# QK-normalized attention and a PReLU MLP on one core: visits by batch replaced by one flat list of bursts

## The chip, the cores and the metric

One Trainium2 chip, one core. The metric is the time of one execution in device microseconds. Engines are named as the profile names them: PE is TensorE (PEld its weight loads), DVE is VectorE, ACT is ScalarE, POOL is GpSimd, SP is SyncE, which here only requests DMAs.

## The reference

```python
def rmsnorm(x, g):
    rms = np.sqrt(np.mean(x * x, axis=-1, keepdims=True) + 1e-06)
    return x / rms * g
q_n, k_n = (rmsnorm(q, g_q), rmsnorm(k, g_k))       # q, k, v: (8, 12, 448, 64)
scores = scale * np.matmul(q_n, k_n.transpose(0, 1, 3, 2))
scores = scores - np.max(scores, axis=-1, keepdims=True)
attn = np.exp(scores)
attn = attn / (np.sum(attn, axis=-1, keepdims=True) + 1e-09)
x = np.matmul(attn, v)      # heads of a token side by side: (3584, 768)
h = x @ w_in                # (768, 2048)
g = np.maximum(h, 0.0) + alpha * np.minimum(h, 0.0)
out = g @ w_out             # (2048, 768), float32
```

## The kernel before

Eight batches, and in each three **pairs**: a pair i holds heads 2i and 2i+1 and the two beside them in the other half of the heads, so four heads, two in each half of the partitions. Keys and tokens are cut into seven tiles of 64 (J = 7).

For a pair, `load_qk` fetches q and k (tile nat, SP's queue), `norm_sum` squares them (tile sq, GpSimd; in batch 0 ACT) and sums on VectorE (tile ss), `norm_root` takes the inverse root on ACT (tile rr), `norm_scale` multiplies (tile qs, GpSimd; in batch 0 VectorE), and `turn` transposes seven blocks on TensorE into PSUM (tile tps) and copies them on VectorE to qT or kT; the gain goes into kT's copy. `score` makes one tile of scores for four heads (tile sc, four matmuls, two PSUM buffers) and its exp on ACT (tile expT). `den` adds the exps of a pair up with ones (tile dn, 28 matmuls) and inverts by Ln and Exp on ACT (tile rden); `attv` makes the values (tile av, 28 matmuls) and VectorE multiplies them by rden into xT. tps, dn and av share one PSUM buffer of two banks (tag acc).

The MLP of a batch is 16 **ups** (`up`: six matmuls into tile hT, alpha times h on ACT into ah, the larger of both on VectorE into gT) and, for two batches together, 14 **downs** (`down`: 16 matmuls over gT into tile op, a copy on VectorE to osb, after every second one an output DMA on SP). hT and op share two PSUM buffers of one bank (tag mm). gT holds two batches side by side.

Each engine runs its instructions in the order in which they are written; the schedule is by hand. A batch is 15 visits. In a visit stand first the preparation of the next batch (list `before`), then denominators or values and up to two score tiles with their exps, then units of the MLP of the batch before, ups first and downs after them, doled out by their estimated cost (1.13 and 2.6). The weights are requested on GpSimd's queue in batch 0, cast from float32 on the way: w_in in six pieces of 128 rows, w_out in 16. After the last batch stand its 16 ups, and after them 8 downs.

## Time and profile before

| | us |
|---|---|
| median of 3 runs | 589.3 |
| lowest and highest | 586.72, 590.89 |
| the profiled execution | 587.75 |
| its span, first to last instruction | 586.0 |
| TensorE busy in it | 459.7 (78%) |
| ACT, VectorE, GpSimd busy | 286.5, 221.6, 164.1 |

The span is what the trace shows; the profiled execution's own time lies 1.75 us above it. A busy TensorE is not one at its peak: the end of a matmul is modelled, and matmuls overlap.

### The profile page before, as it was taken

The page shows a single profiled execution, that of the slowest core. Times are in us where ns is not written, and L with a number is a line of the kernel's source. Part 1 is how long each engine was busy: PE and PEld are TensorE (multiplying, and loading weights), DVE is VectorE, ACT ScalarE, POOL GpSimd, SP SyncE. Part 2 cuts the span into 40 slices and gives each one's busy share as a digit, 9 for nine tenths or more (in the row PEclk, how much of TensorE's full clock was granted, in tenths as well). Part 3 has the DMA queues.
Part 4 walks back from the last instruction along what each step waited for, and adds up shares of the span by engine and source line. Part 5 has one row for each costly group of instructions (what it writes and reads, how often), then busy time and mean ns, then how long its engine had stood idle before and what let it go on. Part 6 is the DMA issues. An engine that isn't in the chain of part 4 may idle for free.

```text
span 586.0 us, 9396 instructions
## 1 busy us (share of the span) xinstructions
PE 459.7 (78%) x4016; PEld 241.5 (41%) x4016; DVE 221.6 (38%) x314; ACT 286.5 (49%) x371; POOL 164.1 (28%) x128
## 2 busy tenths in 40 slices
PE   0232668988698985988969886988969889999996
PEld 0111343455244552445424552445424554455453
DVE  0374326532353223533254323543254223422431
ACT  2245358841565424753557415664367426862410
POOL 2166814520435004360164202560054300000000
PEclk9999899999889998999989998899989999999999
DMA  9999920311930119302443127401363121012013
GB/s 178 218 204 183 250 58 2 48 28 28 213 51 12 44 32 212 49 1 55 113 106 46 28 55 173 81 11 31 93 148 49 29 55 27 3 27 53 3 28 81
DMA packets 30298, 45.45 MB, mean 78 GB/s; under 512 B 5424, under 2 KB 25904, under 8 KB 30256
## 3 DMA queue, kind: packets, MB, share of 16 engines
q1 hardware_dynamic: 20688, 33.05, 23.5%
q0 software_dynamic: 9568, 11.80, 12.4%
q8 instruction: 31, 0.51, 0.4%
q14 instruction: 11, 0.09, 0.1%
HBM read 45.62 MB, written 11.01 MB: 97 GB/s over the span
## 4 chain that ended last, share of the span: by engine, by line
PE 52%; DVE 17%; ACT 11%; DMA 9%; SPq 5%; issue 3%; POOL 2%; POOLq 0%; DVEq 0%; ACTq 0%
PE op L250 26%; PE hT L233 12%; DMA nat<-in_k_dram 7%; DVE ss L120 5%; ACT expT L186 5%; PE dn L197 5%; ACT ah L241 5%; DVE gT L242 4%; PE av L215 4%; SPq L89 4%; PE tps L155 3%; PE sc L179 2%; DVE qT L162 2%; DVE osb L260 2%; POOL sq L119 2%
## 5 line engine op out<-in xcount | busy, mean ns | idle before, releaser
L186 ACT ACTIVATE expT<-sc,expb 128x896 f16<-128x896 f32 x168 | 160.1, 1002 | 86.8 <-PE sc L179 86.8
L233 PE MATMUL hT<-xT,w_in_sb 128*128 128x448 f16 x768 | 165.6, 367 | 39.6 <-DVE gT L242 38.6
L250 PE MATMUL op<-w_out_sb,gT 128*128 128x384 f16 x896 | 153.5, 326 | 2.2 <-DVE gT L242 2.2
L119 POOL TENSOR_TENSOR sq<-nat 128x896 f32<-128x896 f32 x42 | 70.1, 1678 | 237.5 <-DMA nat<-in_q_dram 188.6
L233 PEld LDWEIGHTS <-w_in_sb 128*128 128x128 f16 x768 | 75.0, 100 | 125.3 <-issue 69.5
L242 DVE TENSOR_TENSOR gT<-hT,ah 128x448 f16<-128x448 f32 x128 | 77.4, 622 | 110.5 <-ACT ah L241 109.4
L241 ACT ACTIVATE ah<-hT,alpha_sb 128x448 f16<-128x448 f32 x128 | 79.4, 635 | 70.8 <-PE hT L233 69.3
L250 PEld LDWEIGHTS <-gT 128*128 128x128 f16 x896 | 84.2, 98 | 69.0 <-issue 16.9
L142 POOL TENSOR_TENSOR qs<-nat,rr 128x896 f16<-128x896 f32 x42 | 70.9, 1712 | 60.3 <-ACT rr L134 42.0
L260 DVE COPY osb<-op 128x384 f32<-128x384 f32 x56 | 31.2, 558 | 146.9 <-PE op L250 146.9
L155 PE MATMUL tps<-ident,qs 128*128 128x128 f16 x336 | 29.1, 232 | 61.1 <-DVE qs L142 40.8
L205 ACT ACTIVATE rden<-dn 128x896 f32<-128x896 f32 x24 | 22.0, 917 | 92.3 <-PE dn L197 92.3
L120 DVE TENSOR_REDUCE ss<-sq 128x14 f32<-128x896 f32 x48 | 50.4, 1079 | 36.8 <-POOL sq L119 36.7
L179 PE MATMUL sc<-qT,kT 64*64 64x448 f16 x672 | 54.3, 381 | 5.5 <-ACT expT L186 4.7
L155 PEld LDWEIGHTS <-qs 128*128 128x128 f16 x336 | 23.3, 103 | 68.3 <-DVE qs L142 44.5
L197 PE MATMUL dn<-expT,ones 64*64 64x448 f16 x672 | 39.1, 370 | 10.9 <-DVE kT L164 10.9
L215 PE MATMUL av<-expT,vt 64*64 64x448 f16 x672 | 38.0, 364 | 2.1 <-ACT rden L205 1.3
L224 DVE TENSOR_TENSOR xT<-av,rden 128x896 f16<-128x896 f32 x24 | 26.1, 1089 | 26.6 <-PE av L215 26.6
L179 PEld LDWEIGHTS <-kT 64*64 64x64 f16 x672 | 18.2, 109 | 34.4 <-issue 27.8
L197 PEld LDWEIGHTS <-ones 64*64 64x64 f16 x672 | 22.1, 111 | 23.0 <-issue 13.9
L215 PEld LDWEIGHTS <-vt 64*64 64x64 f16 x672 | 18.9, 109 | 19.1 <-issue 10.0
L206 ACT ACTIVATE rden<-rden 128x896 f32<-128x896 f32 x24 | 22.8, 951 | 0.8
(20 smaller groups left out, 77.9 us busy)
## 6 DMA issues: line engine op xcount, KB each, us to landing
nat<-in_q_dram SPq DMA_DIRECT2D x48, 224.0 KB, 6.2
nat<-in_k_dram SPq DMA_DIRECT2D x48, 224.0 KB, 6.5
out_dram<-osb SPq DMA_DIRECT2D x56, 192.0 KB, 2.7
vt<-in_v_dram POOLq DMA_DIRECT2D x16, 336.0 KB, 5.4
w_in_sb<-in_moe_w_in_dram POOLq DMA_DIRECT2D x6, 512.0 KB, 9.5
w_out_sb<-in_moe_w_out_dram POOLq DMA_DIRECT2D x16, 192.0 KB, 8.4
gain<-in_g_q_dram SPq DMA_DIRECT2D x2, 0.2 KB, 10.1
gk<-in_g_k_dram SPq DMA_DIRECT2D x2, 0.2 KB, 10.3
```

The costliest lines, as they stand in the source:

```text
L119: nc.gpsimd.tensor_mul(out=sqf, in0=src, in1=src)
L120: nc.vector.tensor_reduce(out=ss[:, at].rearrange("p h j -> p (h j)").unsqueeze(2), in_=sq, axis=AXIS_X, op=ALU.add,)
L142: eng.tensor_mul(out=t.rearrange("p j h d -> p h j d"), in0=nat[b, i, nm], in1=rr[:, at].unsqueeze(3).broadcast_to((128, 2, J, D)),)
L155: nc.tensor.transpose(tp[:, j, :], src[:, j].rearrange("p h d -> p (h d)"), ident)
L179: nc.tensor.matmul(out=sc[ds(64 * g, 64), par, :S], lhsT=kT[ds(64 * par, 64), g, j, :], rhs=qT[ds(64 * par, 64), g].rearrange("p j c -> p ...
L186: nc.scalar.activation(out=expT[b, i][:, j], in_=sc[:, :, :S], func=AF.Exp, scale=QK_SCALE, bias=expb[:, 0:1],)
L197: nc.tensor.matmul(out=dn[ds(64 * par, 64), g, :S], lhsT=ones[ds(64 * g, 64), :], rhs=e[ds(64 * g, 64), j, par, :], start=(j == 0), stop=( ...
L215: nc.tensor.matmul(out=av[ds(64 * par, 64), g, :S], lhsT=vt[b][ds(64 * g, 64), 2 * i + par, j, :], rhs=e[ds(64 * g, 64), j, par, :], start ...
L233: nc.tensor.matmul(out=hT[:, :S], lhsT=w_in_sb[:, c, ts(ft, 128)], rhs=x[:, c, :], start=(c == 0), stop=(c == KM - 1),)
L241: nc.scalar.activation(out=ah, in_=hT[:, :S], func=AF.Copy, scale=alpha_sb[:, ft : ft + 1])
L242: nc.vector.tensor_max(out=gT[:, ft, ds((b & 1) * S, S)], in0=hT[:, :S], in1=ah)
L250: nc.tensor.matmul(out=op[:, :OH], lhsT=gT[:, ft, ts(t, 128)], rhs=w_out_sb[:, ft, ds(oh * OH, OH)], start=(ft == 0), stop=(ft == NF - 1),)
```

## The change

The loops over batches and visits go. There are 24 pairs y in one line, 168 score tiles, and 84 **bursts** n. A burst holds, in this order: preparation due at n; the scores of tiles 2n and 2n+1; the exp of the first; denominators or values, if due (denominators one burst after the pair's last score tile, values two after); a turn, if due; then the burst's **gap**, a list of ups and downs. The exp of the second tile, and with denominators the inversion, are written behind the gap's first up, or at the gap's end if it has none. Loads stand 12 bursts ahead of the pair's first scores, squares 6, reduces 5, the root 4, the scale 3, the turn 1. `turn` makes q and k in the two banks of one buffer. In the MLP downs stand between ups, evenly spread. Of a pair of batches' downs, six are done in the odd batch's period and eight in the next one's; after the last burst stand 16 ups and 14 downs. In batch 0 GpSimd scales k, VectorE q. w_in is requested in four pieces of 512 columns, w_out in four of 512 rows.

```diff
-    def load_qk(b, i):
+    def load_qk(y):
+        b, i = divmod(y, G)
         for nm in "qk":
-            t = ld.tile([128, 2, J, D], FP32, name="nat", tag="nat", bufs=8)
+            t = ld.tile([128, 2, J, D], FP32, name="nat", tag="nat", bufs=6)
             for g in range(2):
...
-            nat[b, i, nm] = t
+            nat[y, nm] = t
...
+    def load_w_in(c):
+        nc.gpsimd.dma_start(
+            out=w_in_sb[:, :, ts(c, FB)],
+            in_=moe_w_in[:, ts(c, FB)].rearrange("(k p) f -> p k f", p=128),
+        )
+
+    def load_w_out(c):
+        nc.gpsimd.dma_start(
+            out=w_out_sb[:, ts(c, NF // 4), :],
+            in_=moe_w_out[ts(c, DF // 4), :].rearrange("(t p) m -> p t m", p=128),
+        )
+
+
+    def square(y, nm):
+        src = nat[y, nm].rearrange("p h j d -> p (h j d)")
         sq = ld.tile([128, 2 * J, D], FP32, name="sq", tag="sq", bufs=2)
         sqf = sq.rearrange("p n d -> p (n d)")
-        if fast:
+        if y < G:
             nc.scalar.activation(out=sqf, in_=src, func=AF.Square)
         else:
             nc.gpsimd.tensor_mul(out=sqf, in0=src, in1=src)
+        sqs[y, nm] = sq
+
+    def reduce(y, nm):
+        if nm == "q":
+            ss_t[y] = ld.tile([128, 2, 2, J], FP32, name="ss", tag="ss", bufs=4)
         nc.vector.tensor_reduce(
-            out=ss[:, at].rearrange("p h j -> p (h j)").unsqueeze(2),
-            in_=sq, axis=AXIS_X, op=ALU.add,
-        )
-
...
+    def root(y):
+        rr = ld.tile([128, 2, 2, J], FP32, name="rr", tag="rr", bufs=4)
+        nc.scalar.activation(out=rr, in_=ss_t[y], func=AF.Ln, scale=1.0 / D, bias=epsb[:, 0:1])
         nc.scalar.activation(out=rr, in_=rr, func=AF.Exp, scale=-0.5)
-        rr_t[key] = rr
-
...
+    def scale(y, nm):
         t = ld.tile([128, J, 2, D], FP16, name="qs", tag="qs", bufs=4)
-        eng = nc.vector if fast else nc.gpsimd
+        eng = nc.vector if y < G and nm == "q" else nc.gpsimd
         eng.tensor_mul(
             out=t.rearrange("p j h d -> p h j d"),
-            in0=nat[b, i, nm],
-            in1=rr[:, at].unsqueeze(3).broadcast_to((128, 2, J, D)),
-        )
...
+        qs[y, nm] = t
+
+    def turn(y):
 
         ps = psa.tile([128, 2, 512], FP32, name="tps", tag="acc")
-        tp = ps[:, 0, : S].bitcast(FP16).rearrange("p (j c) -> p j c", j=J)
-        src = qs[b, i, nm]
...
+        for n, nm in enumerate("qk"):
+            tp = ps[:, n, : S].bitcast(FP16).rearrange("p (j c) -> p j c", j=J)
+            for j in range(J):
+                nc.tensor.transpose(
+                    tp[:, j, :], qs[y, nm][:, j].rearrange("p h d -> p (h d)"), ident
+                )
+            t = att.tile([128, 2, J, 64], FP16, name=f"{nm}T", tag=f"{nm}T", bufs=3)
+            o = t.rearrange("p g j c -> p j g c")
+            i4 = tp.rearrange("p j (g c) -> p j g c", g=2)
...
+            qkT[y, nm] = t
...
+    def score(y, j):
+        qT, kT = qkT[y, "q"], qkT[y, "k"]
         sc = pss.tile([128, 2, 512], FP32, name="sc", tag="sc")
...
+        scs[y, j] = sc
+
+    def soft(y, j):
+        if j == 0:
+            expT[y] = att.tile([128, J, 2, S], FP16, name="expT", tag="expT")
         nc.scalar.activation(
-            out=expT[b, i][:, j], in_=sc[:, :, :S], func=AF.Exp,
...
+    def over_keys(name, y, weights):
+        acc = psa.tile([128, 2, 512], FP32, name=name, tag="acc")
...
+        return acc
+
+    def den(y):
+        dn = over_keys("dn", y, lambda g, par, j: ones[ds(64 * g, 64), :])
+        rden[y] = dn
+
+    def invert(y):
         r = att.tile([128, 2, S], FP32, name="rden", tag="rden")
-        nc.scalar.activation(out=r, in_=dn[:, :, :S], func=AF.Ln)
...
+        rden[y] = r
+
+    def attv(y):
+        b, i = divmod(y, G)
+        vv = vt[b]
+        av = over_keys("av", y, lambda g, par, j: vv[ds(64 * g, 64), 2 * i + par, j, :])
...
+    NB = (NG * J + 1) // 2
+
+    def last(y):
+        return (J * y + J - 1) // 2
+
+    dens = {last(y) + 1: y for y in range(NG)}
+    avs = {last(y) + 2: y for y in range(NG)}
+    prep = {}
+
+    def at(n, f, *a):
+        prep.setdefault(max(int(n), 0), []).append((f, a))
+
+    for y in range(G, NG):
+        n = J * y / 2
+        at(n - 12, load_qk, y)
+        for nm in "qk":
+            at(n - 6, square, y, nm)
+            at(n - 5, reduce, y, nm)
+        at(n - 4, root, y)
+        for nm in "qk":
+            at(n - 3, scale, y, nm)
+    for b in range(1, B):
+        at(J * G * b / 2 - 4, load_v, b)
+    turns = {J * y // 2 - 1: y for y in range(1, NG)}
+
+    UP, DOWN = 1.13, 2.6
+
+    def merge(ups, downs):
+        res, done = [], 0
+        for n, u in enumerate(ups):
+            while done < len(downs) and done * len(ups) <= n * len(downs):
+                res.append(downs[done])
+                done += 1
+            res.append(u)
+        return res + downs[done:]
+
+    periods = []
+    for b in range(B):
+        ups = [(UP, up, (b, ft)) for ft in range(NF)]
+        lead, downs = [], []
+        if b > 0 and b % 2 == 0:
+            lead = [(DOWN, down, (b - 2, 3, oh)) for oh in range(2)]
+            downs = [(DOWN, down, (b - 2, t, oh)) for t in range(4, J) for oh in range(2)]
+        elif b > 0:
+            downs = [(DOWN, down, (b - 1, t, oh)) for t in range(3) for oh in range(2)]
+        periods.append(lead + merge(ups, downs))
+    gaps = [[] for _ in range(NB + 2)]
+    for b in range(B - 1):
+        lo = last(G * b + G - 1) + 2
+        hi = last(G * b + 2 * G - 1) + 2
+        total = sum(u[0] for u in periods[b])
+        done, n = 0.0, lo
+        for u in periods[b]:
+            gaps[min(lo + int(done / total * (hi - lo) + 0.3), hi - 1)].append(u[1:])
+            done += u[0]
+    rest = [u[1:] for u in periods[B - 1]]
+    rest += [(down, (B - 2, t, oh)) for t in range(3, J) for oh in range(2)]
...
+    def prepare(y):
+        for nm in "qk":
+            square(y, nm)
+            reduce(y, nm)
+        root(y)
+        for nm in "qk":
+            scale(y, nm)
+
+    prepare(0)
+    nc.vector.tensor_mul(out=gain, in0=gain, in1=gk2)
+    turn(0)
+    prepare(1)
     load_v(0)
-    def prep_fast(i):
...
-        visits = [[] for _ in range(15)]
-        for i in range(G):
-            for n in range(4):
-                for j in range(2 * n, min(2 * n + 2, J)):
-                    visits[4 * i + n].append((score, (b, i, j)))
-            visits[4 * i + 5].insert(0, (den, (b, i)))
-            visits[4 * i + 6].insert(0, (attv, (b, i)))
-        visits[13] = [(den, (b, G - 1))]
-        visits[14] = [(attv, (b, G - 1))]
...
+    at(1, prepare, 2)
+    for c in range(4):
+        at(1 + c // 2, load_w_in, c)
+        at(8 + 2 * c, load_w_out, c)
+
+    for n in range(NB + 2):
+        for f, a in prep.get(n, ()):
+            f(*a)
+        tiles = [divmod(m, J) for m in (2 * n, 2 * n + 1) if m < NG * J]
+        for t in tiles:
+            score(*t)
+        if tiles:
+            soft(*tiles[0])
+        if n in dens:
+            den(dens[n])
+        if n in avs:
+            attv(avs[n])
+        late = [(soft, t) for t in tiles[1:]]
+        if n in dens:
+            late.append((invert, (dens[n],)))
+        if n in turns:
+            turn(turns[n])
+        for f, a in gaps[n]:
+            f(*a)
+            if f is up and late:
+                for g, c in late:
+                    g(*c)
+                late = []
+        for g, c in late:
+            g(*c)
+    for f, a in rest:
+        f(*a)
```

The gaps of 22 bursts, worked out from this code (U an up, D a down, both with no number; den, av, turn: what else the burst holds beside its two score tiles); bursts 23 to 43 repeat three times to the end:

```
12 av U U | 13 turn U | 14 den U U | 15 av U | 16 turn U U | 17 U U | 18 den U
19 av U U | 20 turn U | 21 den U U | 22 av D
23 turn U U U | 24 D | 25 den U U U | 26 av D | 27 turn U U D | 28 den U
29 av U U D | 30 turn U U | 31 U D | 32 den U U | 33 av D D | 34 turn D
35 den U U U | 36 av D U | 37 turn U U D | 38 U U D | 39 den U U | 40 av U D
41 turn U U U | 42 den D U U | 43 av D
```

On ACT, where a period of ups begins (batch 2 of before). hT, ah and rows of alpha belong to ups, sc and expT to score tiles, the number behind a name tells buffers apart:

```order
L186 ACTIVATE expT_1392<-sc_1393,expb_79 128x896
L186 ACTIVATE expT_1392<-sc_1399,expb_79 128x896
L241 ACTIVATE ah_1412<-hT_1405,alpha_sb_92 128x448
L241 ACTIVATE ah_1422<-hT_1415,alpha_sb_92 128x448
L241 ACTIVATE ah_1432<-hT_1425,alpha_sb_92 128x448
L186 ACTIVATE expT_1392<-sc_1442,expb_79 128x896
L186 ACTIVATE expT_1392<-sc_1448,expb_79 128x896
L241 ACTIVATE ah_1461<-hT_1454,alpha_sb_92 128x448
```

and in the new order, bursts 18 and 19, each with one or two ups:

```order
L193 ACTIVATE expT_941<-sc_961,expb_79 128x896
L246 ACTIVATE ah_1008<-hT_1001,alpha_sb_92 128x448
L193 ACTIVATE expT_941<-sc_966,expb_79 128x896
L219 ACTIVATE rden_1012<-dn_972 128x896
L220 ACTIVATE rden_1012<-rden_1012 128x896
L193 ACTIVATE expT_941<-sc_1024,expb_79 128x896
L246 ACTIVATE ah_1072<-hT_1065,alpha_sb_92 128x448
L193 ACTIVATE expT_941<-sc_1029,expb_79 128x896
```

Before, both exps of a visit stand together and the ups' steps behind them; now an up's step stands between the two exps, and in a burst with denominators the inversion (rden) stands behind the second.

On VectorE, a period of a batch before (ss<-sq is a reduce for the next batch, gT the end of an up, osb the end of a down):

```order
L224 TENSOR_TENSOR xT<-av,rden 128x2x448
L260 COPY osb<-op 128x384
L242 TENSOR_TENSOR gT<-hT,ah 128x448 x3
L120 TENSOR_REDUCE ss<-sq 128x14 x2
L242 TENSOR_TENSOR gT<-hT,ah 128x448 x4
L120 TENSOR_REDUCE ss<-sq 128x14 x2
L242 TENSOR_TENSOR gT<-hT,ah 128x448 x5
L120 TENSOR_REDUCE ss<-sq 128x14 x2
L242 TENSOR_TENSOR gT<-hT,ah 128x448 x2
L224 TENSOR_TENSOR xT<-av,rden 128x2x448
L242 TENSOR_TENSOR gT<-hT,ah 128x448 x2
```

and now, from burst 29 to burst 33:

```order
L229 TENSOR_TENSOR xT<-av,rden 128x2x448
L247 TENSOR_TENSOR gT<-hT,ah 128x448 x2
L265 COPY osb<-op 128x384
L132 TENSOR_REDUCE ss<-sq 128x14 x2
L166 COPY qT<-tps 128x7x2x64
L168 TENSOR_SCALAR kT<-tps,gain 128x7x2x64
L247 TENSOR_TENSOR gT<-hT,ah 128x448 x3
L265 COPY osb<-op 128x384
L247 TENSOR_TENSOR gT<-hT,ah 128x448 x2
L132 TENSOR_REDUCE ss<-sq 128x14 x2
L229 TENSOR_TENSOR xT<-av,rden 128x2x448
```

Three pairs of reduces between 14 gT have become one pair in every three or four bursts, and osb stands among gT.

On GpSimd, the start of the program before (vt, w_in_sb, w_out_sb are DMA requests):

```order
L98 DMA vt<-in_v_dram 64x6x448 x2
L330 DMA w_in_sb<-in_moe_w_in_dram 128x2048 x2
L119 TENSOR_TENSOR sq<-nat 128x896 x2
L330 DMA w_in_sb<-in_moe_w_in_dram 128x2048 x4
L119 TENSOR_TENSOR sq<-nat 128x896 x2
L339 DMA w_out_sb<-in_moe_w_out_dram 128x768 x6
L119 TENSOR_TENSOR sq<-nat 128x896 x2
L339 DMA w_out_sb<-in_moe_w_out_dram 128x768 x6
```

and now:

```order
L146 TENSOR_TENSOR qs<-nat,rr 128x2x7x64 x2
L101 DMA vt<-in_v_dram 64x6x448 x2
L146 TENSOR_TENSOR qs<-nat,rr 128x2x7x64
L107 DMA w_in_sb<-in_moe_w_in_dram 128x6x512 x4
L126 TENSOR_TENSOR sq<-nat 128x896 x2
L101 DMA vt<-in_v_dram 64x6x448 x2
L146 TENSOR_TENSOR qs<-nat,rr 128x2x7x64 x2
L126 TENSOR_TENSOR sq<-nat 128x896 x2
L113 DMA w_out_sb<-in_moe_w_out_dram 128x4x768 x2
```

The requests for v and w_in have moved behind the scales of k (qs) for the first two and the third pair.

## Rows read from the trace of the kernel before

**Rows 1.** Two stretches parted at the first up matmul: busy time by engine, clock, DMA.

```profile
0.00:87.80 87.80, 31.74 (x345) 18.47 (x345) 32.25 (x37) 33.99 (x43) 39.78 (x46) 0.96 0.89 182
87.80:586.00 498.20, 427.95 (x3676) 223.02 (x3672) 189.35 (x278) 252.54 (x329) 124.27 (x82) 0.97 0.27 59
```

**Rows 2.** What TensorE waited for from 87.8 us on: us, times, longest.

```profile
PE hT L233 <- DVE gT L242: 38.6, 36, 6.6
...
PE tps L155 <- DVE qT L162: 14.2, 18, 0.8
...
PE dn L197 <- DVE kT L164: 9.3, 12, 0.8
```

**Rows 3.** Head in order of time: start, us, engine, line, operation [idle before, releaser].

```profile
6.08 0.95 ACT L117 ACTIVATE sq<-nat 128x896 f32<-128x896 f32 x1 [4.07 <-DMA nat<-in_q_dram]
...
11.21 0.95 ACT L117 ACTIVATE sq<-nat 128x896 f32<-128x896 f32 x1 [4.17 <-DMA nat<-in_k_dram]
...
16.29 0.16 DVE L275 TENSOR_TENSOR gain<-gain,gk 128x1 f32<-128x1 f32 x1 [15.29 <-DMA gk<-in_g_k_dram]
...
16.37 2.07 DVE L120 TENSOR_REDUCE ss<-sq 128x14 f32<-128x896 f32 x2
...
20.23 0.93 PE L155 MATMUL tps<-ident,qs 128*128 128x128 f16 x7 [20.23 <-DVE qs L142]
...
24.20 3.70 ACT L186 ACTIVATE expT<-sc,expb 128x896 f16<-128x896 f32 x4 [5.15 <-PE sc L179]
```

**Rows 4.** One stretch of the head, columns as in group 1.

```profile
20.00:40.00 20.00, 5.87 (x48) 3.58 (x52) 10.99 (x12) 6.14 (x8) 12.01 (x14) 1.00 1.00 198
```

**Rows 5.** Order of time, middle of the program, downs between attention work.

```profile
394.36 1.52 PE L197 MATMUL dn<-expT,ones 64*64 64x448 f16 x28 [0.78 <-DVE kT L164]
...
395.68 0.57 PE L179 MATMUL sc<-qT,kT 64*64 64x448 f16 x8
...
400.24 0.55 PE L179 MATMUL sc<-qT,kT 64*64 64x448 f16 x8
...
400.72 2.77 PE L250 MATMUL op<-w_out_sb,gT 128*128 128x384 f16 x16
...
403.33 0.55 PE L155 MATMUL tps<-ident,qs 128*128 128x128 f16 x7
```

**Rows 6.** Order of time, ups in the tail.

```profile
538.67 2.43 PE L233 MATMUL hT<-xT,w_in_sb 128*128 128x448 f16 x12
...
540.01 0.63 ACT L241 ACTIVATE ah<-hT,alpha_sb 128x448 f16<-128x448 f32 x1 [6.08 <-PE hT L233]
...
540.68 0.62 DVE L242 TENSOR_TENSOR gT<-hT,ah 128x448 f16<-128x448 f32 x1 [1.24 <-ACT ah L241]
...
541.14 0.63 ACT L241 ACTIVATE ah<-hT,alpha_sb 128x448 f16<-128x448 f32 x1 [0.50 <-PE hT L233]
...
541.36 2.43 PE L233 MATMUL hT<-xT,w_in_sb 128*128 128x448 f16 x12 [0.25 <-DVE gT L242]
```

**Rows 7.** Order of time, the last copy of the output.

```profile
581.09 0.56 DVE L260 COPY osb<-op 128x384 f32<-128x384 f32 x1 [2.04 <-PE op L250]
```

**Rows 8.** Groups of instructions by line: busy us, mean ns, idle before.

```profile
L186 ACT ACTIVATE expT<-sc,expb 128x896 f16<-128x896 f32 x168 | 160.1, 1002 | 86.8 <-PE sc L179 86.8
...
L206 ACT ACTIVATE rden<-rden 128x896 f32<-128x896 f32 x24 | 22.8, 951 | 0.8
...
L205 ACT ACTIVATE rden<-dn 128x896 f32<-128x896 f32 x24 | 22.0, 917 | 92.3 <-PE dn L197 92.3
```

**Rows 9.** Order of time, start of a period.

```profile
364.33 1.08 DVE L120 TENSOR_REDUCE ss<-sq 128x14 f32<-128x896 f32 x1 [1.03 <-POOL sq L119]
...
366.00 4.06 PE L233 MATMUL hT<-xT,w_in_sb 128*128 128x448 f16 x12 [5.54 <-DVE gT L242]
```

**Rows 10.** Two stretches, columns as in group 1: ordinary ups, ups after an idle.

```profile
100.00:150.00 50.00, 43.69 (x432) 23.92 (x425) 19.31 (x30) 27.08 (x35) 14.11 (x10) 1.00 0.20 39
...
366.00:369.00 3.00, 3.00 (x9) 1.23 (x9) 0.47 (x1) 0.56 (x1) 2.83 (x2) 0.50 0.99 220
```

More of the change, by code (lines that the diff above doesn't have):

```diff
@@ L46 @@
     W = 2 * S
+    NG = B * G
+    FB = DF // 4
     cst = ctx.enter_context(tc.tile_pool(name="cst", bufs=1))
@@ L170 @@
-    expT, rden = {}, {}
-    def score(b, i, j):
-        if j == 0:
-            expT[b, i] = att.tile([128, J, 2, S], FP16, name="expT", tag="expT")
-        qT, kT = qkT[b, i, "q"], qkT[b, i, "k"]
+        for n, nm in enumerate("qk"):
[7 more added lines that the diff above has]
+            i4 = tp.rearrange("p j (g c) -> p j g c", g=2)
+            if nm == "q":
+                nc.vector.tensor_copy(out=o, in_=i4)
+            else:
+                nc.vector.tensor_scalar(
+                    out=o, in0=i4, scalar1=gain[:, 0:1], scalar2=None, op0=ALU.mult
+                )
+            qkT[y, nm] = t
@@ L176, in score @@
+    expT, rden, scs = {}, {}, {}
+    def score(y, j):
+        qT, kT = qkT[y, "q"], qkT[y, "k"]
         sc = pss.tile([128, 2, 512], FP32, name="sc", tag="sc")
@@ L197, in den @@
                     nc.tensor.matmul(
-                        out=dn[ds(64 * par, 64), g, :S],
-                        lhsT=ones[ds(64 * g, 64), :],
+                        out=acc[ds(64 * par, 64), g, :S],
+                        lhsT=weights(g, par, j),
                         rhs=e[ds(64 * g, 64), j, par, :],
@@ L203, in den @@
                     )
+        return acc
[3 more added lines that the diff above has]
+    def invert(y):
         r = att.tile([128, 2, S], FP32, name="rden", tag="rden")
-        nc.scalar.activation(out=r, in_=dn[:, :, :S], func=AF.Ln)
+        nc.scalar.activation(out=r, in_=rden[y][:, :, :S], func=AF.Ln)
         nc.scalar.activation(out=r, in_=r, func=AF.Exp, scale=-1.0)
-        rden[b, i] = r
-    def attv(b, i):
-        av = psa.tile([128, 2, 512], FP32, name="av", tag="acc")
-        e = expT[b, i]
-        for j in range(J):
-            for g in range(2):
-                for par in range(2):
-                    nc.tensor.matmul(
-                        out=av[ds(64 * par, 64), g, :S],
-                        lhsT=vt[b][ds(64 * g, 64), 2 * i + par, j, :],
-                        rhs=e[ds(64 * g, 64), j, par, :],
-                        start=(j == 0),
-                        stop=(j == J - 1),
-                    )
+        rden[y] = r
[3 more added lines that the diff above has]
+        av = over_keys("av", y, lambda g, par, j: vv[ds(64 * g, 64), 2 * i + par, j, :])
         if i == 0:
@@ L224, in attv @@
         nc.vector.tensor_mul(
-            out=xT[b][:, :, i, :], in0=av[:, :, :S], in1=rden[b, i]
+            out=xT[b][:, :, i, :], in0=av[:, :, :S], in1=rden[y]
         )
@@ L270 @@
         nc.sync.dma_start(out=gk2[ds(64 * g, 64)], in_=g_k.unsqueeze(1))
-    load_qk(0, 1)
-    load_qk(0, 2)
+    load_qk(1)
+    load_qk(2)
     nc.sync.dma_start(out=alpha_sb, in_=moe_alpha.rearrange("(t p) -> p t", p=128))
-    load_v(0)
-    nc.vector.tensor_mul(out=gain, in0=gain, in1=gk2)
-    def prep_fast(i):
-        for nm in "qk":
-            norm_sum(0, i, nm, True)
-        norm_root(0, i, True)
-        for nm in "qk":
-            norm_scale(0, i, nm, True)
-        for nm in "qk":
-            turn(0, i, nm)
```

112 lines of the change are left out of this document (10 added, 102 removed).

## Prediction

> **What bounds the kernel now.** I parted the execution at the first matmul of the MLP's first half, an "up", at 87.8 us [rows 1]. Before it TensorE is busy 31.7 of 87.8 us while the DMA engines are busy 0.89 of the time; after it TensorE is busy 428.0 of 498.2 us and DMA 0.27. So there are two kernels here: a head that waits, and a long part in which TensorE is the bound and loses 70 us.
>
> The table of waits says for what TensorE waits in the long part [rows 2]: 38.6 us before ups, for gT of an earlier up (that frees the up's PSUM buffer); 14.2 us in the middle of a turn, where k's transposes wait for q's copy; 9.3 us where denominators wait for k's copy. All three are waits for VectorE on buffers of PSUM.
>
> In the head I read the rows in order of time [rows 3]. q of pair 0 is squared at 6.08 us, k only at 11.21, 4.17 us late by its DMA; the gain product holds VectorE until 16.29, so the two reduces behind it start at 16.37 although k's square ended at 12.16; transposes at 20.23, first exps at 24.20. The DMA engines are full meanwhile [rows 4], because GpSimd requests v and a third of w_in while q and k are still to come.
>
> Now the price of dense work, read as the distance from one start to the next where nothing waits [rows 5]: 28 matmuls of denominators 1.32 us (394.36 to 395.68), a pair of score tiles 0.48 (400.24 to 400.72), a down 2.61 (400.72 to 403.33), seven transposes about 0.5 (0.55 with their tail). An up is 1.13: of two in a row the second's ACT step starts 1.13 after the first's [rows 6]. The whole program holds 128 ups (144.6), 56 downs (146.2), 84 pairs of score tiles (40.3), 48 sets of denominators or values (63.4), 48 half turns (24): 418.5 us. What is done before the first up is 10.5 pairs, 6 sets and 12 half turns (18.9) now, and will be 13 pairs, 6 sets and 8 half turns (18.1): 400 us of dense work stand behind the first up in both. From the last matmul to the end it is 5.1 us: the last copy starts at 581.09, 0.2 after its matmuls [rows 7]. So before is 87.8 + 400 + 5 = 493, and **93 us of its 586.0 are waits behind the first up** (65 of them plain idle, the rest half-speed matmuls and the refilling of the pipeline after each wait).
>
> **The change, part by part.** *Head.* GpSimd now scales k of pairs 0 and 1 before it requests v, and k of pair 2 before w_in, so q and k of batch 0 have the DMA engines alone. The least: k's square follows q's at 7.0, 4.2 us earlier, and without the gain's hold the reduces start 5.2 us earlier than k's square allowed, exps at 14.8; but ACT now also does pair 1's root ahead of the first exp, for which two reduces of 1.08 and the two small root steps (together 0.6, an estimate from ACT's other rows) must pass, so 17.5. The most: the gain's DMAs, issued at the same place, land as late as now, at 16.29; two copies (1.3) and the same 2.7 behind it give 20.4. I take 18.5. Then ACT sets the pace up to burst 12: 24 exps at 0.93 [rows 3], three inversions of 0.92 + 0.95 [rows 8], pair 2's two squares (1.9) with its reduce and root (1.7), two more roots (1.2): 32.7, then a pair of scores and the values (1.8): 53. TensorE is at its lower clock level there by its durations (seven transposes in 0.93 at 20.23 against 0.55 later [rows 3, 5]), though the granted clock shows 1.00; if it stays there, its 13 pairs, 6 sets and 8 half turns take 36 instead of 18 us and press on ACT: up to 60. Bounds 50 to 60, **first up at 54** instead of 87.8. w_in's first quarter must be there by then: at 198 GB/s [rows 4] 10 MB can have moved, and q and k of three pairs, v, two later pairs and that quarter are about 7.
>
> *Squares and reduces.* Today a load, its square and its reduce are handed out within two visits. At 364.33 VectorE stands at a reduce, waiting for GpSimd, which waited for a DMA; two gT stand behind it, and TensorE idles 5.54 us; the two ups after that take 4.06 instead of 2.44 [rows 9], because the granted clock is at 0.50, the lower level [rows 10]. Five period starts show the same, with 3.8 to 6.6 us of idle. Now loads go out 12 bursts ahead, squares 6 and reduces 5. Even in the full head k's first load had landed by 11.21 [rows 3]; six bursts are 30 us. So these waits go whole, and nothing takes their place on VectorE: a reduce's square is a burst old.
>
> *Turn.* q and k are turned into two banks of one buffer, so k's 14 us of waits for q's copy go, and units stand behind a turn, not denominators, which takes the 9 us.
>
> *Ups between downs, exps between ups.* Here the new waits come. An up's buffer is free 1.56 us after its end: 0.21 to ACT, 0.63, 0.04, 0.62 on VectorE, 0.06 back [rows 6]. With two buffers a unit directly behind two ups waits 1.56 - 1.13 = 0.43. In the 21 bursts of two batches (the list of gaps) that is 8 times: 3.4 us. **The late exp** is what the change adds: the second tile's exp stands behind the first up's ACT step. It ends 0.21 + 0.63 + 1.00 = 1.84 after that up, and the next burst's second score tile wants its buffer 0.24 after the gap's end. If the first up is also the gap's last unit (bursts 28, 36) TensorE waits 1.6: 3.2; if one up follows (bursts 30, 32, 39, 42), 0.47, four times: 1.9. In a denominator burst the Ln stands behind that late exp too and ends 2.8 after the first up; the values that need its buffer then wait 0.7, four times: 2.8. Twice a second up's ACT step stands behind both inversion steps and the next down waits 0.6: 1.1. Together 12 us for two batches, three times 12. The first period, ups alone, has four lone ups (6.4), four of the 0.47 kind and four of the 0.7 kind: 11. In the tail five triples of ups: 2. **Waits behind the first up 50** instead of 93. The least is half of them (25), if exps and evictions slip into other gaps; the most 80, if the waits of one burst carry into the next.
>
> *Without cost:* six downs go from the middle into the tail, dense in both; 14 more root steps on ACT (0.6 each) lie where ACT has room: two batches, some 115 us, hold 42 exps of 1.00, 32 ACT steps of ups of 0.63 and 12 inversion steps of 0.93 [rows 6, 8], 73 us. SP's outputs stand behind far-ahead loads, which wait for a scale one or two bursts earlier; three output buffers cover that.
>
> **Sum:** 54 + 400 + 50 + 5 = 509 us of span. The profiled execution has 587.75 for 586.0 of span, so 511; it lies 1.5 below the median of 589.3, which I leave out.
>
> **The rivals.** *ACT becomes the bound of the bursts.* Exp, up, exp, up in one queue could string each burst along ACT, and as much wait would stand behind the first up as now, 93: 54 + 400 + 93 + 5 + 2 = 554. For: every gap has its exp behind an up. Against: ACT's 73 us of 115, above.
>
> *The weights come late.* w_in is requested only when pair 2 is scaled, some 24 us in, in rows of 2 KB instead of 8. If that halved the rate, the first up would stand at 70 to 88: 527 to 545. Against: only a quarter is needed at first.
>
> *Slower: the clock falls.* The new order breaks TensorE's work into bursts with a short wait in nearly each; if the granted clock then went to its lower level, each us of dense work would cost another. From 80 us of such work on, a fifth of the 400, the gain is gone and the kernel is slower: at a third, 511 + 133 = 644. Against: in 100 to 150 us, where ups wait for gT by fractions of a us, 1.00 was granted [rows 10], and 0.50 came after an idle of over 5 us. The Trainium skill (TensorE: Matmul & The Clock Gate, "A second HAM failure mode: psum-queue depth-cycling") tells of a kernel whose short idles between groups of matmuls, as it cycled through PSUM, did make the clock swing; by this rule the rival would hold, and this trace does not agree with it at waits under 1 us.
>
> *Better:* 25 us of waits and a first up at 50 give 482.
>
> **How the numbers follow.** Chances: forecast with its bounds (486 to 536) 0.74; ACT-bound 0.08; late weights 0.08; better 0.05; slower 0.04; none of these, within 1%, 0.01. The range reaches to half of the late weights, 486 to 540. The runs of before lie 0.7% apart, so 1% is about what a measurement can tell. Faster by over 1% holds in all but the last two: 0.95, same 0.01, slower 0.04.
>
> **What would show it.** First up near 54, with k's first square right behind q's; no reduce that holds gT; no wait inside a turn; 58 us for each batch in the middle; among TensorE's waits the largest new entry scores for expT, some 20 to 25 us in all, then values for rden; a granted clock of 1.00 from 60 us on. I am wrong if scores wait for exps in bursts with several ups, if ups wait for w_in, or if the clock dips in the middle.

## The result and the profile after

| | before | after | forecast |
|---|---|---|---|
| median, us | 589.3 | **552.0** | 511 |
| lowest, highest | 586.7, 590.9 | 550.2, 555.2 | 486 to 540 |
| profiled execution, its span | 587.75, 586.0 | 552.83, 551.1 | 511, 509 |
| first up | 87.8 | 58.4 | 54 |

The ratio is 0.938 [0.932, 0.943]: the change gains 37 us of the 78 that were forecast, and the time lies above the range. Two stretches of the changed kernel, parted at its first up (columns as in [rows 1]):

```profile
0.00:58.40 58.40, 29.48 (x329) 15.55 (x330) 24.82 (x29) 37.36 (x48) 33.30 (x30) 0.91 1.03 209
58.40:551.10 492.70, 431.77 (x3692) 225.45 (x3688) 192.97 (x282) 253.78 (x352) 130.96 (x87) 0.98 0.30 67
```

Most of the gain lies in the head: of the 34.9 us by which the profiled span is shorter, 29.4. The long part is 492.7 us where it was 498.2. What TensorE waited for in it (us, times, longest):

```profile
PE tps L159 <- DVE qT L166: 25.3, 20, 2.2
PE sc L181 <- ACT expT L193: 16.1, 27, 1.3
PE av L204 <- ACT rden L219: 6.3, 15, 0.4
PE hT L238 <- DVE gT L247: 3.5, 14, 0.2
PE op L255 <- DVE gT L247: 2.7, 11, 0.2
```

Beside [rows 2]: the 38.6 us for gT are 3.5, the 9.3 of denominators are gone, the 14.2 inside turns are 25.3, and scores now wait for exps. TensorE is idle for 60.9 us here; 5 of them are the end after the last matmul, which leaves 56 us of waits. Its 431.8 busy us are 32 more than the 400 of dense work that the prediction counted, so by the prediction's way of counting 56 + 32 = 88 us of waits lie behind the first up, where 93 did.

The head in order of time, against [rows 3] (for each line start, us, [idle before, releaser]):

```profile
7.20 0.95 ACT L124 ACTIVATE sq<-nat 128x896 f32<-128x896 f32 x1 [0.72 <-DMA nat<-in_k_dram]
...
10.92 1.64 DVE L352 TENSOR_TENSOR gain<-gain,gk 128x1 f32<-128x1 f32 x1
...
11.06 0.93 PE L159 MATMUL tps<-ident,qs 128*128 128x128 f16 x7 [11.06 <-DVE qs L146]
...
17.28 1.89 ACT L193 ACTIVATE expT<-sc,expb 128x896 f16<-128x896 f32 x2
...
58.39 0.55 PE L238 MATMUL hT<-xT,w_in_sb 128*128 128x448 f16 x2
```

k's square follows at 7.20 (11.21 before), the first transposes stand at 11.06 (20.23), the first exps at 17.28 (24.20).

Then a turn with two reduces due in its burst, and the ups behind it:

```profile
110.73 0.56 PE L159 MATMUL tps<-ident,qs 128*128 128x128 f16 x7
110.81 2.07 DVE L132 TENSOR_REDUCE ss<-sq 128x14 f32<-128x896 f32 x2
112.80 0.62 DVE L166 COPY qT<-tps 128x896 f16<-128x896 f16 x1
113.47 0.55 PE L159 MATMUL tps<-ident,qs 128*128 128x128 f16 x7 [2.17 <-DVE qT L166]
...
113.85 5.25 PE L238 MATMUL hT<-xT,w_in_sb 128*128 128x448 f16 x18
```

q's transposes end at 111.29, but VectorE is at the reduces until 112.8; then comes q's copy, and only then k's transposes, 2.17 us late. Of the 20 turns behind the first up six wait 2.17 us, three 1.40 us behind reduces that had begun earlier, and eleven 0.7 to 0.8 us. One of these eleven, with no reduces in its burst, shows the same order with a shorter wait:

```profile
134.07 0.62 DVE L166 COPY qT<-tps 128x896 f16<-128x896 f16 x1 [0.18 <-PE tps L159]
...
134.75 0.55 PE L159 MATMUL tps<-ident,qs 128*128 128x128 f16 x7 [0.72 <-DVE qT L166]
```

The three ups behind the long wait take 5.25 us where dense ones take 3.4 (1.13 each). Windows of 2 us over that place (columns as in [rows 1]) show why: TensorE was busy 0.53 of 2 us, and then the lower clock level was granted for most of the next 4 us (1.00 again from 118 us on).

```profile
112.00:114.00 2.00, 0.53 (x8) 0.49 (x8) 1.41 (x2) 0.00 (x0) 0.00 (x0) 1.00 0.00 0
114.00:116.00 2.00, 2.00 (x9) 0.88 (x7) 0.68 (x1) 0.21 (x1) 0.00 (x0) 0.60 0.00 0
116.00:118.00 2.00, 2.00 (x8) 0.80 (x7) 0.62 (x1) 1.32 (x2) 0.00 (x0) 0.55 0.00 0
```

That doesn't follow each such wait. Of the six of 2.17 us, the lower level came after two (at 113.47 and 370.11) and not after the other four (156.14, 241.90, 283.30, 412.78). The first of the four, with the stretch around it:

```profile
156.14 0.55 PE L159 MATMUL tps<-ident,qs 128*128 128x128 f16 x7 [2.17 <-DVE qT L166]
156.53 2.43 PE L238 MATMUL hT<-xT,w_in_sb 128*128 128x448 f16 x12
```

```profile
150.00:160.00 10.00, 7.44 (x60) 3.91 (x60) 5.21 (x9) 4.07 (x7) 0.00 (x0) 1.00 0.00 0
```

The late exp, at the place that the prediction named (a denominator burst with one up):

```profile
143.58 0.38 PE L181 MATMUL sc<-qT,kT 64*64 64x448 f16 x4
145.27 0.38 PE L181 MATMUL sc<-qT,kT 64*64 64x448 f16 x4 [1.31 <-ACT expT L193]
146.07 1.52 PE L204 MATMUL av<-expT,vt 64*64 64x448 f16 x28 [0.42 <-ACT rden L219]
```

A pair of score tiles that isn't parted takes 0.57 (at 119.04, for one); parted it takes 0.38 twice, 0.19 more, beside the idle.

### The profile page after: what moved, and what is told of

It is laid out like the page before. It is cut to its first block, busy times and chain, and to the rows that moved or that the text cites. A ratio compares the mean times of both kernels' runs of the same rounds, so it can differ in the third digit from the quotient of the medians.

```text
span 551.1 us, 9402 instructions
## 1 busy us (share of the span) xinstructions
PE 461.2 (84%) x4016; PEld 241.0 (44%) x4016; DVE 217.8 (40%) x311; ACT 291.1 (53%) x399; POOL 164.3 (30%) x117
## 4 chain that ended last, share of the span: by engine, by line
PE 63%; ACT 15%; DVE 13%; issue 3%; DMA 3%; SPq 2%; DVEq 0%
PE op L255 26%; PE hT L238 19%; ACT ah L246 6%; PE dn L204 6%; ACT expT L193 6%; DVE ss L132 5%; PE av L204 5%; PE sc L181 4%; PE tps L159 4%; DVE gT L247 4%; ACT rden L219 3%; DVE qT L166 3%; DMA nat<-in_k_dram 2%; SPq L92 1%; DVE xT L229 1%
## 5 line engine op out<-in xcount | busy, mean ns | idle before, releaser
L193 ACT ACTIVATE expT<-sc,expb 128x896 f16<-128x896 f32 x168 | 164.3, 1002 | 62.6 <-PE sc L181 62.5
L146 POOL TENSOR_TENSOR qs<-nat,rr 128x896 f16<-128x896 f32 x45 | 77.8, 1747 | 269.0 <-ACT rr L140 267.7
L247 DVE TENSOR_TENSOR gT<-hT,ah 128x448 f16<-128x448 f32 x128 | 79.4, 624 | 189.8 <-ACT ah L246 189.8
L255 PEld LDWEIGHTS <-gT 128*128 128x128 f16 x896 | 86.5, 98 | 69.1 <-issue 13.7
L181 PE MATMUL sc<-qT,kT 64*64 64x448 f16 x672 | 58.4, 386 | 28.1 <-ACT expT L193 26.0
L181 PEld LDWEIGHTS <-kT 64*64 64x64 f16 x672 | 16.8, 107 | 66.7 <-issue 62.0
L204 PE MATMUL av<-expT,vt 64*64 64x448 f16 x672 | 36.3, 351 | 8.0 <-ACT rden L219 8.0
L204 PEld LDWEIGHTS <-vt 64*64 64x64 f16 x672 | 22.3, 106 | 20.3 <-issue 12.9
L168 DVE TENSOR_SCALAR kT<-tps,gain 128x896 f16<-128x896 f16 x24 | 16.4, 683 | 17.5 <-PE tps L159 17.5
```

Source lines behind the costliest of these rows:

```text
L146: eng.tensor_mul(out=t.rearrange("p j h d -> p h j d"), in0=nat[y, nm], in1=rr_t[y][:, "qk".index(nm)].unsqueeze(3).broadcast_to((128, 2, ...
L181: nc.tensor.matmul(out=sc[ds(64 * g, 64), par, :S], lhsT=kT[ds(64 * par, 64), g, j, :], rhs=qT[ds(64 * par, 64), g].rearrange("p j c -> p ...
L193: nc.scalar.activation(out=expT[y][:, j], in_=scs[y, j][:, :, :S], func=AF.Exp, scale=QK_SCALE, bias=expb[:, 0:1],)
L204: nc.tensor.matmul(out=acc[ds(64 * par, 64), g, :S], lhsT=weights(g, par, j), rhs=e[ds(64 * g, 64), j, par, :], start=(j == 0), stop=(j == ...
L247: nc.vector.tensor_max(out=gT[:, ft, ds((b & 1) * S, S)], in0=hT[:, :S], in1=ah)
L255: nc.tensor.matmul(out=op[:, :OH], lhsT=gT[:, ft, ts(t, 128)], rhs=w_out_sb[:, ft, ds(oh * OH, OH)], start=(ft == 0), stop=(ft == NF - 1),)
```

## Experiments

**Both halves of a turn before the copies.** All 14 transposes are written first, then q's copy and k's, on the changed kernel.

```diff
+        tps = {}
         for n, nm in enumerate("qk"):
             tp = ps[:, n, : S].bitcast(FP16).rearrange("p (j c) -> p j c", j=J)
+            tps[nm] = tp
             for j in range(J):
                 nc.tensor.transpose(
                     tp[:, j, :], qs[y, nm][:, j].rearrange("p h d -> p (h d)"), ident
                 )
+        for nm in "qk":
+            tp = tps[nm]
             t = att.tile([128, 2, J, 64], FP16, name=f"{nm}T", tag=f"{nm}T", bufs=3)
```

> The changed kernel, with the fourteen transposes of q and k of a turn written ahead of the two copies. Theory A (the loss is that k's transposes wait for q's copy, and the clock falls behind the long ones): the 25.3 us of TensorE's waits for q's copy after the first up go, with the refilling behind each (20 times 0.17) and some five stretches at the lower clock level (about 2 us each): 552 - 25 - 3 - 10 = 514 us, 508 to 524. Rival B (the wait only moves: VectorE holds the pair's copies, so denominators, values or ups' evictions come late instead): under 10 us of gain, 542 to 552, and a new entry of more than 10 us in TensorE's table of waits.

Measured: 517.95 us, 0.878 [0.874, 0.881], so 34 us below the changed kernel; first up at 55.4. TensorE's largest waits behind it:

```profile
PE sc L185 <- ACT expT L197: 15.6, 27, 1.3
PE av L208 <- ACT rden L223: 6.3, 15, 0.4
PE hT L242 <- DVE gT L251: 5.1, 16, 0.6
```

Theory A's range holds it. The turn's waits are gone whole, and the scores' and values' have stayed. At one turn, the two reduces that held k's transposes now stand beside an up:

```profile
104.27 0.95 PE L161 MATMUL tps<-ident,qs 128*128 128x128 f16 x14
104.35 2.07 DVE L132 TENSOR_REDUCE ss<-sq 128x14 f32<-128x896 f32 x2
...
105.06 2.43 PE L242 MATMUL hT<-xT,w_in_sb 128*128 128x448 f16 x12
106.33 0.61 DVE L170 COPY qT<-tps 128x896 f16<-128x896 f16 x1
```

Idle behind the first up fell by 23.1 us (60.9 to 37.8), busy time by 8.9 (431.8 to 422.9), the head by 3.0. The clock is most of the 8.9: the shortfall of the granted clock, summed over stretches of 10 us from 60 us to the last matmul, is 10.2 us in the changed kernel, in five places, and 3.4 here, in two. The 14 transposes also take 0.95 where two sevens took 0.55 and 0.56.

**Only the reduces moved.** In the changed kernel a burst's reduces are written behind its turn; q's copy still stands ahead of k's transposes.

```diff
         for f, a in prep.get(n, ()):
-            f(*a)
+            if f is not reduce:
+                f(*a)
...
             turn(turns[n])
+        for f, a in prep.get(n, ()):
+            if f is reduce:
+                f(*a)
```

> The changed kernel, with a burst's two reduces written behind its turn's copies on VectorE instead of ahead of them; q and k of a turn still one after the other. Theory A: the waits of 2.17 us for q's copy (a reduce pair of 2.07 stands ahead of it) become 0.72 like the others, 10 times 1.45 = 15 us, and the lower clock level no longer appears in the middle (about 10 us): 527 us, 522 to 533. Rival C (the clock falls for another reason, such as many short waits): 537, with the granted clock still at 0.5 to 0.6 in places. Rival B: no gain, 545 to 552.

Measured: 545.56 us, 0.924 [0.919, 0.928]: 6.4 of the 25 expected, which lies in rival B's range (545 to 552). The expectation had counted ten waits of 2.17 us, where there are six, and three of 1.40. The trace is of the fastest of the four runs, 542.04; the others took 545.3 to 546.1. Its waits behind the first up, here at 62.2:

```profile
PE tps L159 <- DVE qT L166: 14.9, 20, 1.1
PE hT L238 <- DVE gT L247: 6.9, 20, 1.0
...
PE op L255 <- DVE gT L247: 5.0, 14, 1.0
```

So of the 25.3 us in the turn some 10 are the reduces ahead of q's copy and 15 are the copy itself. The granted clock is 1.00 from 70 us to the last matmul in this run; over the whole program its mean is 0.990 here and 0.976 to 0.981 in the other three, so in them the clock was lower for longer. And the reduces now hold gT (3.4 us more before ups, 2.3 before downs), and the first up stands 3.8 us later: in the head scores wait 12.8 us for exps, 9.9 in the changed kernel, since ACT's root waits for the later reduce, ahead of the exps.

**The same turn in the kernel before.** q and k of a pair in two banks of one buffer, all transposes first; `turn` is rewritten as in the first experiment and called once for a pair.

```diff
-                    before[9 + 2 * i].append((turn, (nb, i, nm)))
+                before[9 + 2 * i].append((turn, (nb, i)))
```

> The kernel before, with q and k of a pair turned in the two banks of one buffer, all transposes ahead of both copies; nothing else. Theory A (what the turn's waits are worth there): 14.2 us of waits for q's copy go with their refilling, denominators behind a turn wait some 3 us more: 589 - 12 = 577 us, 570 to 582. Rival J (the waits all go over to the denominators and nothing is gained): 585 to 592.

Measured: 580.77 us, 0.984 [0.980, 0.987], first up 88.5. As expected the turn's 14.2 us go, and part of them comes back before denominators (9.3 us become 15.7), which stand right behind the turn there. The waits for gT stay at 38.6.

**Exps in pairs.** In the changed kernel both exps stand ahead of the denominators, and only the inversion stays behind the first up.

```diff
-        if tiles:
-            soft(*tiles[0])
+        for t in tiles:
+            soft(*t)
...
-        late = [(soft, t) for t in tiles[1:]]
+        late = []
```

> The changed kernel, with both exps of a burst written one after the other on ACT, the first up's step behind them (the inversion still behind the first up). Theory A (late exps cost what the table of waits shows, 16.6 us of scores waiting for exps and some 5 of refilling; early ones make the ups' steps later by up to 1 us in bursts that begin with an up): scores' waits gone, ups' and downs' waits for gT up from 6 to 10 or 20, 540 to 555. Rival D (ACT's order is what bounds the bursts): over 20 us of gain, under 532.

Measured: 534.26 us, 0.905 [0.901, 0.909], between the two theories' times. The waits for exps fell from 16.1 to 0.2 us; those in turns grew to 30.1. The groups of score matmuls of the changed kernel and of this one (busy us, mean ns | idle before):

```profile
L181 PE MATMUL sc<-qT,kT 64*64 64x448 f16 x672 | 58.4, 386 | 28.1 <-ACT expT L193 26.0 <-DVE kT L168 2.1
```

```profile
L181 PE MATMUL sc<-qT,kT 64*64 64x448 f16 x672 | 53.4, 382 | 12.4 <-ACT expT L193 10.4 <-DVE kT L168 2.1
```

So besides the idle, 5.0 us of busy time go: 27 pairs that were parted, at 0.19 each, are 5.1. Evictions of ups hardly suffer: their waits for gT rose by 0.6 us, those of downs by 1.4. The clock is not part of this gain: its shortfall from 60 us to the last matmul is 10.2 us here too.

**Both repairs.** The two edits together.

> The changed kernel with both edits: the transposes of q and k ahead of the copies, and both exps of a burst together ahead of the first up's ACT step. Theory A (two losses side by side; the first was worth 34 us alone, the second 18): most of the second is left, 518 - 15 = 503 us, 498 to 508. Rival F (with the turn mended the exps are hidden, or the ups' evictions take their place): 512 to 520.

Measured: **494.73 us, 0.839 [0.836, 0.841]**, the best of all and below the ranges of both theories. From 55.1 us on:

```profile
55.10:492.90 437.80, 413.58 (x3692) 219.93 (x3688) 191.00 (x283) 255.36 (x352) 130.98 (x88) 1.00 0.34 78
```

```profile
PE op L259 <- DVE gT L251: 6.8, 14, 1.4
PE hT L242 <- DVE gT L251: 5.5, 16, 0.6
PE av L208 <- ACT rden L223: 4.5, 5, 1.0
```

Against the turn alone, the pairs are worth 23 us: 13.6 of idle, 4.5 of score matmuls, 3.4 of clock (up to the last matmul no stretch of 10 us is below 1.00 any more), the rest smaller groups. With them 33 us of waits are left behind the first up (437.8 - 400 - 5).

**All three.** The reduces behind the turn as well.

> The changed kernel with transposes ahead of copies, exps in pairs, and the reduces behind the turn. Theory A (reduces ahead of a turn cost only through TensorE's wait inside the turn, which is gone): within 1% of 494.7, 490 to 499. Rival M (VectorE's queue still sets when gT and copies come): 483 to 489, or over 500 where reduces now stand ahead of gT.

Measured: 507.40 us, 0.860 [0.858, 0.863]. It is rival M's second case. Once k's transposes wait for no copy, the reduces do little harm ahead of the turn (with both repairs TensorE waits 0.8 us behind the first up for k's copy), and behind it they stand ahead of gT:

```profile
PE hT L242 <- DVE gT L251: 12.4, 20, 1.6
```

12.7 us are lost: 5.9 in the head, where scores wait 15.9 us for exps instead of 10.5, and 6.9 for gT of ups.

**Ups first, then downs.** In the changed kernel the units of a period are no longer mixed.

```diff
-        periods.append(lead + merge(ups, downs))
+        periods.append(lead + ups + downs)
```

> The changed kernel, with the ups of a period all ahead of its downs (as before) instead of mixed; the two downs that must come first stay. Theory A (downs between ups hide the chain over ACT and VectorE): waits of ups for gT from 3.5 to 20 us or more, exps later in bursts of ups alone, 565 to 580 us. Rival I (with attention work in every burst the mixing is worth nothing): 548 to 556.

Measured: 556.07 us, 0.944 [0.940, 0.948]: the mixing is worth 4 us (0.7%), no more than the spread of the kernel's runs; that is at the upper end of rival I's range. The waits of scores for exps fall to 7.9 us here, and those inside turns grow to 31.4.

```profile
PE hT L238 <- DVE gT L247: 7.8, 29, 0.4
```

The waits for gT are 7.8 us, not the 38.6 of [rows 2]: what removed those is not the mixing. The squares and reduces long behind their loads are the part of the change that is left for it, and the traces fit that: from 60 us on VectorE waited with a reduce for GpSimd's square ten times in the kernel before, 21.9 us in all, and never in the changed kernel or in this one. That part was not undone by itself.

**The head: weights first.** In the changed kernel GpSimd requests v and all of w_in before anything else.

```diff
+    load_v(0)
+    for c in range(4):
+        load_w_in(c)
     prepare(0)
```

> The changed kernel, with v of batch 0 and all four pieces of w_in requested on GpSimd at the very start, ahead of the scales of k. Theory A (q and k gain from having the DMA engines alone): k of pair 0 squared at 11 instead of 7.2 us, pairs 1 and 2 later by the time that v and w_in take, first up at 70 to 85 instead of 58: 563 to 578 us. Rival E (the head is bound by ACT and by TensorE at its lower clock level, not by loads): first up within 4 us of 58, time within 1%.

Measured: 554.91 us, 0.941 [0.937, 0.946], first up 62.9. q and k do come later now:

```profile
10.32 0.95 ACT L124 ACTIVATE sq<-nat 128x896 f32<-128x896 f32 x1 [2.93 <-DMA nat<-in_k_dram]
...
22.11 1.89 ACT L193 ACTIVATE expT<-sc,expb 128x896 f16<-128x896 f32 x2
```

The first exps stand 4.8 us later, the first up 4.5; that is far from theory A and just over rival E's 4 us. So the DMA engines that q and k had to themselves are worth 4 or 5 us of the head's 29, and some 3 us of the whole time, which is within the spread of the runs.

**The head: the requests as before.** The changed kernel with w_in in 6 pieces by rows at bursts 0 to 2, w_out in 16 at bursts 3 to 8.

```diff
-        at(1 + c // 2, load_w_in, c)
-        at(8 + 2 * c, load_w_out, c)
+    for j in range(KM):
+        at(j // 2, row_in, j)
+    for ft in range(NF):
+        at(3 + ft // 3, row_out, ft)
```

> The changed kernel, with the weights requested in the pieces and at the places of the kernel before (w_in in six pieces at bursts 0 to 2, w_out in 16 at bursts 3 to 8). Theory K (w_out early fills the DMA engines and GpSimd's queue): first up 8 to 20 us later than 58, 558 to 572 us. Rival L (the order of work on TensorE decides the head): first up within 4 us of 58, 548 to 556.

Measured: 565.39 us, 0.962 [0.956, 0.967], first up 73.6, 15 us later, as theory K had it. The requests stand ahead of GpSimd's scales and squares, and most of them wait for earlier DMAs. Most of the 15 us fall in one turn: q's transposes wait for GpSimd's scale, and then k's for q's copy, which stands behind a reduce that waits for GpSimd's square:

```profile
54.00 0.54 POOL L361 DMA_DIRECT2D w_out_sb<-in_moe_w_out_dram  x1 [0.44 <-DMA w_out_sb<-in_moe_w_out_dram]
...
56.31 0.93 PE L159 MATMUL tps<-ident,qs 128*128 128x128 f16 x7 [7.55 <-POOL qs L146]
...
61.24 1.09 DVE L132 TENSOR_REDUCE ss<-sq 128x14 f32<-128x896 f32 x1 [12.91 <-POOL sq L126]
...
64.55 0.91 PE L159 MATMUL tps<-ident,qs 128*128 128x128 f16 x7 [7.31 <-DVE qT L166]
```

**The head of the kernel before.** Three edits, each on the kernel before: the preparation of pairs 1 and 2 of batch 0 at visit 1; that preparation at visits 1 and 4 with batch 1's steps and w_out later; w_out alone from visit 10 on.

```diff
-            before[2] = [(prep_fast, (1,))]
-            before[6] = [(prep_fast, (2,))]
+            before[1] = [(prep_fast, (1,)), (prep_fast, (2,))]
```

> The kernel before, with pairs 1 and 2 of batch 0 normalized and turned at visit 1, ahead of batch 1's reduces, instead of at visits 2 and 6; nothing else. Theory G (the head of before waits in VectorE's queue: batch 0's pairs stand behind reduces of batch 1, whose loads come late): first up from 87.8 to about 65, 566 us, 558 to 575. Rival H (the head of before waits for the DMA engines, which are full to 80 us): first up still over 82, time within 1% of 589.

```diff
-            before[2] = [(prep_fast, (1,))]
-            before[6] = [(prep_fast, (2,))]
+            before[1] = [(prep_fast, (1,))]
+            before[4] = [(prep_fast, (2,))]
...
+            h = 4 if b == 0 else 0
-                    before[2 * i + 1].append((norm_sum, (nb, i, nm, False)))
+                    before[(5 + i) if h else 2 * i + 1].append((norm_sum, (nb, i, nm, False)))
...
-                    before[9 + 2 * i].append((turn, (nb, i, nm)))
+                    before[(11, 13, 14)[i] if h else 9 + 2 * i].append((turn, (nb, i, nm)))
```

> The kernel before, with the head of batch 0 in an order like that of the changed kernel: pairs 1 and 2 prepared at visits 1 and 4, batch 1's reduces at visits 5 to 7, its root at 8, scales at 9 to 11, turns at 11, 13 and 14, and w_out requested from visit 10 on. Theory K (the head's gain comes from what stands ahead of batch 0's pairs in the queues: batch 1's reduces on VectorE, w_out's requests on GpSimd and on the DMA engines): first up from 87.8 to 62 or so, 564 us, 556 to 572. Rival L (it comes from having fewer turns ahead of the first up, 8 halves against 12, and from bursts): first up over 75, 576 to 587.

```diff
-                before[3 + ft // 3].append
+                before[10 + ft // 4].append
```

> The kernel before, with w_out requested from visit 10 of batch 0 on instead of from visit 3; nothing else. Theory K (the DMA engines, full to 80 us, make batch 1's loads late, and VectorE's reduces of batch 1 hold batch 0's pairs): first up from 87.8 to 72 to 80, 574 to 582 us. Rival L (loads are not what the head waits for): first up over 84, 584 to 591.

Measured: 584.54 us, 0.990 [0.985, 0.994], first up 84.3; 583.09, 0.988 [0.986, 0.991], 82.5; 589.55, 0.999 [0.997, 1.002], 88.3. None brings the head near 58; times and first ups are those of rivals H and L. In the first, the second and third of TensorE's three waits for q's scale come earlier and are shorter (6.33 and 4.50 us for 10.64 and 9.90), and then batch 1's turn waits for GpSimd, which is at w_out's requests until 60.58 and at v's until 62.66:

```profile
31.28 0.93 PE L155 MATMUL tps<-ident,qs 128*128 128x128 f16 x7 [6.33 <-DVE qs L142]
...
38.33 0.93 PE L155 MATMUL tps<-ident,qs 128*128 128x128 f16 x7 [4.50 <-DVE qs L142]
...
64.43 0.93 PE L155 MATMUL tps<-ident,qs 128*128 128x128 f16 x7 [4.69 <-POOL qs L142]
```

In the second, without such a wait, 70 to 80 us runs at the lower clock level (granted 0.50): three turns, one after the other, with their copies and a wait for the inversion, stand ahead of the first up.

## Why the prediction was wrong

**The step that failed: "q and k are turned into two banks of one buffer, so k's 14 us of waits for q's copy go."** They became 25.3 us. That k has its own bank frees nothing when q's copy is written ahead of k's transposes into the same buffer: k's still wait for it, as the releaser in the rows says. Written the other way round the wait is gone and 34 us with it. The sentence was taken from the two banks, not from the order of instructions.

**"Nothing takes their place on VectorE"**, said of the reduces, fell with it. A reduce no longer waits for its square, true; but two of them, 2.07 us, stand ahead of q's copy where both fall into one burst, as the listing of VectorE's new order ahead of the prediction already had it. That is 10 of the 25.3 us, as the run with the reduces moved shows (14.9 left). What formerly held gT holds a turn.

**Waits behind the first up: 50 forecast, 88 measured, 56 with the turn mended** (516.1 - 55.4 - 400 - 5). With that one step mended the kernel takes 518 against 511, within the range. That it comes so near is in part luck. The 50 were added up from idle times alone, and the mended kernel idles only 32.8 us there (37.8 less the end). The other 22.9 are TensorE's busy time above the 400, of which 3.4 go to the clock and 5.1 to parted score tiles; the rest was not taken apart. For this the sum had no term, although its 93 for the kernel before held 28 of the kind; in the changed kernel it is 32, and 13.6 are left with both repairs. One term too large and one left out nearly cancel.

The bounds of the forecast, 486 to 536, don't use the prediction's own extreme either: 80 us of waits give 541. The 88 measured lie outside that too.

**"The late exp"** was right in kind and somewhat too large. Scores were to wait 20 to 25 us for it, and values some 11 (16 times 0.7) for the inversion behind it; 16.1 and 6.3 were measured, with 1.31 the longest where 1.6 was worked out. Its whole price, from the runs without it, is 19 us (551.1 to 531.9 of span) or, beside the mended turn, 23 (516.1 to 492.9), since a pair of score tiles torn in two costs 0.19 of its own, and beside the mended turn the clock fell twice behind a late exp. What it buys, ups evicted a little earlier, shows as 2 us of waits for gT, 3.7 beside the mended turn.

**The slower rival, the clock,** was real at a small scale. With both repairs, where no wait is longer than 1.4 us and few are over 1, the granted clock is 1.00 from 55 us to the last matmul. The changed kernel makes longer ones, and at five places the clock fell: 10 us, not 133. Two of the five stand behind 2.17 us in a turn, three behind 1.31 for an exp followed by 0.71 or 1.40 in a turn. The length of a wait alone doesn't decide it: four waits of 2.17 and one of 1.31 followed by 1.40 (at 77 to 79 us) left the clock at 1.00. With the turn mended it fell twice behind 1.31 followed by 0.42 for values, at 134.70 and 253.58, and two more such places left it at 1.00. The Trainium skill (TensorE: Matmul & The Clock Gate, "A second HAM failure mode: psum-queue depth-cycling") tells of a kernel in which short idles between groups of matmuls made the clock swing. The trace of the changed kernel agrees with it at five places, out of some 90 waits.

**ACT as the bound** gave 554, and the time came out at 552: the right number for another reason. ACT is busy 254 of 493 us, and what hangs on it, the waits for exps and inversions (16.1 + 6.3), is a quarter of the 88; the largest wait is VectorE's.

**The head: 54 forecast, 58.4 measured,** inside the bounds (50 to 60). k's square at 7.0 (7.20), exps at 18.5 (17.28), the lower clock level in part (granted 0.84 in 40 to 50, 0.68 in 50 to 60). The turn's step is in it as well: with the turn mended the first up stands at 55.4. Of the reasons that the prediction gave, q and k alone on the DMA engines is worth 4.5 us only; the other, the gain's product no longer ahead of the reduces, was not undone by itself (in [rows 3] it held them from 12.16 to 16.37). What the traces show of the rest is one entry of TensorE's waits up to the first up, before and after:

```profile
PE tps L155 <- DVE qs L142: 40.8, 3, 20.2
```

```profile
PE tps L159 <- DVE qs L146: 11.1, 1, 11.1
```

It waited for q's scale once for each pair of batch 0, and now for the first alone; the difference, 29.7, is about the head's gain of 29.4 (other waits and the busy time moved too, by up to 5 us each way). Keeping the requests out of the way of GpSimd's scales and squares is necessary for it with this turn (15 us). The order of batch 0's pairs alone isn't enough in the old order of work, where batch 1's three turns come before the first up. How the rest divides among the order of preparation and the number of turns ahead of the first up is not settled.

**Right as told:** the waits for gT (38.6 to 3.5), the denominators' 9.3, the starts of periods, and six downs moved into the tail at no cost (TensorE waits 1.0 us in all from 505 us to the last matmul). The rival of the late weights did not come: no up waits for w_in.

## What to carry to other kernels

In this program a second bank took no wait away as long as the copy out of the first was written ahead of what fills the second: look at the order of instructions, not at the buffers alone. When work is moved, look what stands behind it in its queue at the new place: a pair of reduces of 2.07 us cost 10 us ahead of a copy that TensorE waits for, little where the transposes came first, and 7 us ahead of gT. A wait inside a dense group costs more than its idle: it tears the group in two (0.19 us for a pair of score tiles), and behind some of the longer ones the lower clock level came.
